# Chunk decays as running products on VectorE, in a kernel of a Mamba-2 scan and an ELU feed-forward layer

## The chip, the cores and the metric

The kernel runs on one core of one Trainium2 chip. The metric is the device time of one execution, in microseconds (us). A core has five engines that run side by side[...]: TensorE (PE in the profile, with its weight loads as PEld), VectorE (DVE), ScalarE (ACT), GpSimd (POOL) and SyncE (SP, which here only issues DMAs). Matmul results go to PSUM.

## The reference

Four batches with eight heads each and 768 tokens pass through a state-space scan; its output, 3072 tokens of 256 features, then passes through a feed-forward layer with ELU. All is float32.

```python
# scan, per batch and head, in chunks (32 tokens here; the result does not depend on the chunk)
la   = log(clip(a, 1e-6, 1));  cum = cumsum(la)          # inside the chunk
L    = exp(cum[i] - cum[j]) * (i >= j)
y    = ((C @ B.T) * L) @ x + (C @ state) * exp(cum)[:, None]
state = exp(sum(la)) * state + sum_j exp(cum[-1] - cum[j]) * B[j] x[j]
# feed-forward
h = y @ w_in;  g = where(h > 0, h, exp(min(h, 0)) - 1);  out = g @ w_out
```

Since cum is a running sum of logarithms, exp(cum[i] - cum[j]) is the product of a over the tokens j+1 to i.

## The kernel before

The sequence is cut into 12 blocks of 256 tokens, numbered n = 0 to 11, and each block into four chunks of 64 tokens (u and v, two by two). A block of the scan needs these steps, whose names recur below:

- `spread_cum` loads, for all eight heads, the row of cum from DRAM (`flat`) into every partition of the tile L (128 partitions are two chunks' tokens j; the free axis is head, u, token i). Its load is one of two buffers of L.
- `decay` turns L in place into decays: an ACT exponent with the bias -cum[j] for each head and u (L439; 16 in a block), and a GpSimd select that zeroes i < j (L444; four in a block). Blocks 0 and 1 make their decays in another way (`first_low`, `first_cum`, `first_decays`) and are not touched by the change.
- `scaled` multiplies B by exp(cum[-1] - cum[j]) on GpSimd; `turn` transposes B and C on TensorE and copies and masks them (ACT `bt`, DVE `ctm` L381, `cts` L389).
- `scores` makes C B^T in four PSUM banks, `weigh` (DVE, L468) multiplies it by L, `sums` and `states` carry the state on, `across` and `inside` make y and copy it to the tile yT.

The float64 weights arrive as raw 32-bit words in 16 pieces and are made into float32: `w_abs` (ACT), `w_low` (an ACT or DVE instruction, the second argument of `w_take` says which), `w_sign` and `w_high` (DVE), `w_sum` (GpSimd).

The feed-forward part of blocks 0 to 3 runs as plain matmuls: `l1` (L583) fills a PSUM bank, `elu` frees it again with ACT Relu (L596), ACT Exp (L603) and the DVE instruction g (L605); `l2` (L707) is the second product. From block 4 on blocks go in pairs (n, n+1), and both products are done by a scheme with seven matrix products in place of eight, which needs additions on DVE and GpSimd. For each pair there are eight rounds i, each of two half-rounds k = 2i and 2i+1:

- even k: `front` (three products into two banks c1 and c2), `front_sums` (DVE L673 and L674; L673 needs the ACT copy L665), the ELU of the c2 before it, with a GpSimd subtraction behind it (`sum_t1`, L727), and four steps of the second product (L759) of the pair before;
- odd k: `mid` (two products), the DVE addition L682, two steps of L759, then `back` (two products; the first overwrites what L682 reads), the DVE additions L689 and L690, one more step of L759, the ELU of c1, and the Relu of c2 begun.

Every fourth step of L759 ends a product, and DVE adds it up (L750). At the end of each half-round `scan_ahead` issues the scan's steps of the pair that comes next: among others `turn` at k = 5 and 7. The whole order is written by hand (`manual_schedule`); each engine executes its own instructions in program order, so an instruction that waits holds all that come behind it on its engine. PSUM is a pool of seven banks used in rotation and one bank of its own.

Of the kernel before, what the change touches and what calls it, by code (L numbers as in the profile page):

```python
# [28 lines left out]
def kernel(  # L29
# [233 lines left out]
    make_heads(0)  # L263
    make_heads(1)

    def clip(t):
        nc.vector.tensor_scalar(
            out=t, in0=t, scalar1=1e-6, scalar2=1.0, op0=ALU.max, op1=ALU.min)
# [26 lines left out]
    nc.scalar.activation(E0, E0, ACT.Exp)  # L295

    F = const.tile([ROWS, 2, 2, P], F32, name="F")
    E = la

    def rest_of_sums():  # L300
        to_last(F[:, 0], E, nc.gpsimd)
        nc.scalar.activation(E, E, ACT.Exp)


    flat = tc.dram_tile([2, ROWS, 2, Q], F32, name="flat")
# [22 lines left out]
    state = {}  # L328
    starts = {}

    def spread_cum(n):
# [27 lines left out]
    def scaled(n, eng):  # L359

        s = st[n]
        s["sc"] = sc = att.tile([P, 2, NH, N], F32, tag="sc", name="sc", bufs=3)
        factor = eb0[:, :, NH * n:NH * (n + 1)] if n < 2 else eb[:, :, rows_of(n)]
        eng.tensor_tensor(
            out=sc, in0=s["bc"][:, 0],
            in1=factor.unsqueeze(3).to_broadcast([P, 2, NH, N]), op=ALU.mult)
# [63 lines left out]

    def decay(n, q):

        decay_of(n, 2 * q)
        decay_of(n, 2 * q + 1)

    def decay_of(n, h):
        L, row = st[n]["L"], rows_of(n).start + NG * h
        for u in range(2):
            nc.scalar.activation(  # L439
                L[:, h, u], L[:, h, u], ACT.Exp, bias=ncum[:, u, row:row + 1])  # L440
        if h % 4 == 3:
            for v in range(2):
                part = L[Q * v:Q * v + Q, h - 3:h + 1]
                nc.gpsimd.affine_select(  # L444
                    out=part, in_=part, pattern=[[0, 4], [0, 2], [1, Q]],
                    compare_op=ALU.is_ge, fill=0.0, base=0, channel_multiplier=-1)

# [387 lines left out]
    states(0, most)  # L835
    w_abs(0)
    w_low(0, nc.scalar)
    log_of(la)
    scores(0)
    idle_product(3)  # L840
    weigh(0, 0)
# [17 lines left out]
    w_high_a(1)  # L859
    w_high_b(1)  # L860
    w_sum(1)
    running_sums(la, F[:, 0], ROWS)
    l1(0, 0)
    w_abs(2)
    w_low(2, nc.scalar)
    w_sign(2)
    w_give(2)
    elu()
    nc.scalar.activation(F[:, 1], F[:, 0], ACT.Exp)
    write_flat()  # L870
    spread_cum(2)
    w_load(5)
    load_bc(2)
    w_load(6)
# [11 lines left out]
    turn(1)  # L886
    first_exp(1)
    scaled(1, nc.gpsimd)
    rest_of_sums()
    w_give(3)  # L890
    make_heads(2)
    turn_exp(1)
    l1(0, 2)
    elu()
# [8 lines left out]
    l1(0, 3)  # L903
    inside(across(1), 1)
    w_take(4, nc.vector)
    ncum = turned(F[:, 0], "ncum", -1.0, nc.vector)
    eb = turned(E, "eb", 1.0, nc.vector)
    w_give(4)
    elu()
    load_bc(3)  # L910
# [3 lines left out]
    for s, (n, i) in enumerate((  # L914
            (1, 0), (1, 1), (1, 2), (0, 4), (1, 3), (0, 5), (1, 4), (0, 6), (1, 5), (0, 7),
            (1, 6), (1, 7))):
        l1(n, i)
        if s < 8:
            decay_of(2, s)
        if s == 7:  # L920
            scores(2)
            weigh(2, 0)
            weigh(2, 1)
        if s % 2 == 1 and todo < 10:
            w_take(todo, nc.vector)
            w_give(todo)
            w_load(todo + 6)
            todo += 1
        if s == 4:
            scaled(2, nc.gpsimd)  # L930
        if s == 5:
            turn(2)
            first_exp(2)
            turn_exp(2)
        if s == 8:
            spread_cum(3)
            load_x(3)
            spread_exp(3)
            weigh(2, 2)
            weigh(2, 3)  # L940

            st[0] = kept
            sums(2, 0, pool=p_o, tag="o", parts=(None, last))
            states(0, last)
            st.pop(0)
            states(2)
        if s == 10:
            spread_cum(4)
            inside(across(2), 2)
        if len(lag) > 1:  # L950
            elu()
# [15 lines left out]
    def scan_ahead(n, i):  # L967


        m = n + 2 + n % 2  # L970
        if 4 < m < NP and n % 2 == 1 and i in (4, 5):
            spread_cum(m + i - 4)
        m = n + 2 - n % 2
        if 4 <= m < NP and n % 2 == 0:
            if i < 2:
                load_bc(m + i)
                spread_exp(m + i)
            if i == 2:
                if m == 4:
                    spread_cum(5)  # L980
                load_x(m)
                load_x(m + 1)
            for k in (i,) if m == 4 else (i, i + 1) if i % 2 == 0 else ():
                if k >= 2:
                    decay(m + k // 6, (k - 2) % 4)
            if i in (5, 7):
                turn(m + i // 7)
                turn_exp(m + i // 7)
        if 4 <= m < NP and n % 2 == 1:
            if i == 0:  # L990
                scaled(m, nc.gpsimd)
                scaled(m + 1, nc.gpsimd)
            for k in (i,) if m == 4 else (i, i + 1) if i % 2 == 0 else ():
                if k < 2:
                    decay(m + 1, k + 2)
            if i == 2 and m == 4:
                scores(m, m + 1)
                sums(m, m + 1)
                for q in range(4):
                    weigh(m, q)  # L1000
                    weigh(m + 1, q)
                states(m)
                states(m + 1)
# [7 lines left out]
    for n in (2, 3):  # L1011
        for i in range(8):
            l2(n - 2, i)
            if todo < len(pieces):
                w_take(todo, nc.vector)
            end_of_two(n, 2 * i)
            l1(n, i)
            if todo < len(pieces):
                w_give(todo)
                w_load(todo + 6)  # L1020
                todo += 1
            while lag:
# [24 lines left out]
            end_of_two(n, 2 * i + 1)  # L1047
# [116 lines left out]
```

## Time and profile before

The time of the kernel is 364.41 us, the median of three runs (364.33 to 365.36). The profiled execution spans 362.9 us, so 1.5 us of the median lie around the span.

| what | value |
|---|---|
| span of the profiled execution | 362.9 us |
| PE busy | 354.3 us (98%) |
| DVE busy | 242.2 us (67%), 547 instructions |
| ACT busy | 200.7 us (55%), 499 instructions |
| POOL busy | 227.1 us (63%), 366 instructions |
| L439, the exponents, ACT 128x64 | 160 instructions, 41.0 us busy, 338 ns each |
| L444, the selects, POOL 64x512 | 40 instructions, 27.3 us busy, 682 ns each |
| DVE g (L605), 128x512 | 96 instructions, 681 ns each |

The busy times of engines other than PE add up work that lies beside PE's, so a smaller sum there need not shorten the span. A matmul's record holds its time in the pipeline, and consecutive matmuls overlap; how fast PE goes is better read from the starts. Three stretches are told apart below: up to 53 us (the first two blocks, the weights arriving, `l1` alone), 53 to 117 us (blocks 2 and 3, `l1` and `l2` in turn), and from 117 us on (the pairs 4, 6, 8 and 10, about 56 us each).

### The profile page before, as it was taken

To read this page: it belongs to the slowest core of one execution; us is meant where nothing else is said; L and a number is where in the kernel's file an instruction comes from. 1 tells how busy PE (TensorE), PEld (TensorE's weight loads), DVE (VectorE), ACT (ScalarE), POOL (GpSimd) and SP (SyncE) were. 2 spreads that over 40 slices of the span, in tenths; PEclk is the share of its full clock that TensorE was granted. 3 is DMA by queue.
4 is the path that set the end of the run, shared out by engine and by line. 5 is a ranking of instruction groups with operands and counts; after the bars stand their busy time and mean duration, and the time that the engine had idled before them with its cause. 6 is when DMAs were issued, how large, how long until landed. Compare 5 with 4: busy or idle time off the path is not lost.

```text
span 362.9 us, 10146 instructions
## 1 busy us (share of the span) xinstructions
PE 354.3 (98%) x3978; PEld 316.9 (87%) x3978; DVE 242.2 (67%) x547; ACT 200.7 (55%) x499; POOL 227.1 (63%) x366
## 2 busy tenths in 40 slices
PE   8899999999999999999999999999999999999996
PEld 5578778888888998898999998999989999999995
DVE  4989887972697668784567684666685666666212
ACT  4858969767435567635485735386735352534100
POOL 4454443663567896679457578567587555456893
PEclk9999999999999999999999999999999999999999
DMA  8877995563050560053530045540000100000001
GB/s 155 203 203 147 240 308 141 66 116 63 3 116 19 65 85 12 4 115 48 96 65 2 3 95 68 93 72 0 3 2 4 58 2 0 3 0 32 29 2 58
DMA packets 96239, 25.33 MB, mean 70 GB/s; under 512 B 77312, under 2 KB 92096, under 8 KB 96192
## 3 DMA queue, kind: packets, MB, share of 16 engines
q1 hardware_dynamic: 94016, 24.49, 33.0%
q8 instruction: 31, 0.51, 0.6%
q10 hardware_dynamic: 2176, 0.20, 0.4%
q14 instruction: 16, 0.13, 0.1%
HBM read 21.33 MB, written 3.34 MB: 68 GB/s over the span
## 4 chain that ended last, share of the span: by engine, by line
PE 81%; DVE 7%; ACT 3%; DMA 3%; SPq 2%; issue 2%; POOL 1%; ACTq 0%; DVEq 0%
PE ps_o L759 32%; PE ps_h L655 25%; PE ps_h L583 10%; PE ps_o L707 8%; SPq L112 2%; PE ps_g L459 1%; DMA w<-in_moe_w_in_dram 1%; DVE g L605 1%; PE ps_y L553 1%; ACT e L596 1%; PE ps_st L489 1%; ACT e L603 1%; DMA flat<-F 1%; DVE mag L183 1%; PE ps_y L534 1%
## 5 line engine op out<-in xcount | busy, mean ns | idle before, releaser
L596 ACT ACTIVATE e<-ps_h 128x512 f32<-128x512 f32 x96 | 56.5, 588 | 93.1 <-DVE ps_h L689 71.2
L605 DVE SCALAR_TENSOR_TENSOR g<-e,ps_h 128x512 f32<-128x512 f32 x96 | 65.3, 681 | 39.2 <-ACT e L603 35.8
L759 PEld LDWEIGHTS ps_o<-w_out,g 128*128 128x128 f32 x640 | 80.3, 192 | 3.3 <-issue 0.5
L759 PE MATMUL ps_o<-w_out,g 128*128 128x128 f32 x640 | 81.4, 275 | 0.0
L727 POOL TENSOR_TENSOR g<-g 128x256 f32<-128x256 f32 x34 | 24.8, 729 | 67.1 <-DVE g L605 67.1
L583 PE MATMUL ps_h<-yT,w_in 128*128 128x256 f32 x256 | 60.6, 383 | 2.5 <-POOL w_in L200 1.8
L603 ACT ACTIVATE e<-e 128x512 f32<-128x512 f32 x96 | 60.9, 634 | 2.2
L583 PEld LDWEIGHTS ps_h<-yT,w_in 128*128 128x128 f32 x256 | 47.8, 190 | 10.6 <-POOL w_in L200 2.8
L759 PE MATMUL ps_o<-w_sum,g 128*128 128x128 f32 x320 | 43.0, 275 | 0.0
L759 PEld LDWEIGHTS ps_o<-w_sum,g 128*128 128x128 f32 x320 | 41.1, 192 | 1.4
L439 ACT ACTIVATE L<-L,ncum 128x64 f32<-128x64 f32 x160 | 41.0, 338 | 0.0
L655 PE MATMUL ps_h<-y_sum,w_in 128*128 128x256 f32 x128 | 38.6, 383 | 0.7 <-DVE ps_h L682 0.7
L655 PE MATMUL ps_h<-y_sum,w_sum 128*128 128x256 f32 x128 | 38.5, 382 | 0.5 <-DVE g L605 0.5
L655 PE MATMUL ps_h<-yT,w_in 128*128 128x256 f32 x128 | 38.8, 385 | 0.0
L444 POOL TENSOR_SCALAR_AFFINE_SELECT L<-L 64x512 f32<-64x512 f32 x40 | 27.3, 682 | 13.1 <-ACT L L439 11.8
L707 PE MATMUL ps_o<-w_out,g 128*128 128x256 f32 x128 | 30.8, 383 | 0.0
L655 PEld LDWEIGHTS ps_h<-y_sum,w_sum 128*128 128x128 f32 x128 | 23.9, 190 | 5.3 <-DVE g L605 1.3
L723 POOL TENSOR_TENSOR g<-t,g 128x256 f32<-128x256 f32 x40 | 27.9, 729 | 0.8 <-PE ps_o L759 0.8
L723 POOL TENSOR_TENSOR t<-g 128x256 f32<-128x256 f32 x40 | 28.1, 736 | 0.2
L723 POOL TENSOR_TENSOR g<-g,t 128x256 f32<-128x256 f32 x40 | 27.9, 730 | 0.2
L707 PEld LDWEIGHTS ps_o<-w_out,g 128*128 128x128 f32 x128 | 23.7, 190 | 3.4 <-POOL L L444 0.2
L689 DVE TENSOR_TENSOR ps_h<-ps_h,u_sum 128x256 f32<-128x256 f32 x32 | 13.7, 429 | 18.3 <-PE ps_h L655 18.3
(109 smaller groups left out, 538.3 us busy)
## 6 DMA issues: line engine op xcount, KB each, us to landing
L<-flat SPq DMA_DIRECT2D x20, 256.0 KB, 5.3
w<-in_moe_w_in_dram SPq DMA_DIRECT2D x8, 512.0 KB, 5.2
w<-in_moe_w_out_dram SPq DMA_DIRECT2D x8, 512.0 KB, 6.1
xr<-in_x_dram SPq DMA_DIRECT2D x24, 128.0 KB, 3.4
out_dram<-c_sum SPq DMA_DIRECT2D x10, 256.0 KB, 2.1
bc<-in_B_dram SPq DMA_DIRECT2D x24, 64.0 KB, 4.4
bc<-in_C_dram SPq DMA_DIRECT2D x22, 64.0 KB, 3.4
ec<-flat_exp SPq DMA_DIRECT2D x72, 16.0 KB, 1.7
```

What stands on the lines that cost most here:

```text
L439: nc.scalar.activation(L[:, h, u], L[:, h, u], ACT.Exp, bias=ncum[:, u, row:row + 1])
L444: nc.gpsimd.affine_select(out=part, in_=part, pattern=[[0, 4], [0, 2], [1, Q]], compare_op=ALU.is_ge, fill=0.0, base=0, channel_multiplier=-1)
L583: nc.tensor.matmul(out=ps[:, j], lhsT=w_in[:, k, m * P:(m + 1) * P], rhs=yT[n // 2][:, k, n % 2].rearrange("p u i -> p (u i)"), start=(k = ...
L596: nc.scalar.activation(begun[0], lag[0][2], ACT.Relu, scale=-1.0)
L603: nc.scalar.activation(e, e, ACT.Exp, scale=-1.0)
L605: nc.vector.scalar_tensor_tensor(out=g_of[n, i], in0=e, scalar=1.0, in1=ps, op0=ALU.subtract, op1=ALU.max)
L655: nc.tensor.matmul(out=out, lhsT=lhsT, rhs=rhs, start=first, stop=True, skip_group_check=True)
L689: nc.vector.tensor_tensor(out=c1[:, 1], in0=c1[:, 1], in1=u[:, 0], op=ALU.add)
L707: nc.tensor.matmul(out=o_of[n][:, ts], lhsT=g_of[n, j][:, m % 2, ts * P:(ts + 1) * P], rhs=w_out[:, m], start=(m == 0 and ts == 0), stop=( ...
L723: nc.gpsimd.tensor_tensor(out=out, in0=in0, in1=in1, op=ALU.subtract)
L727: eng.tensor_tensor(out=b12, in0=b12, in1=g_of[n, i][:, 0], op=ALU.subtract)
L759: nc.tensor.matmul(out=ps[:, ts], lhsT=b[:, ts * P:(ts + 1) * P], rhs=a[:, i], start=(i == chunk[0] and ts == 0), stop=(i == chunk[-1]), s ...
```

## The change

From block 2 on the decays are made without logarithms. The tile L now receives the row of a itself, with a zero at the first token of each chunk, and one DVE scan for each pair of heads makes L[i] = L[i-1] * a[i] + same[i], where `same` is one at i = j and zero elsewhere. So the value is zero before j, one at j, and the product of a from j+1 to i after it; the zero at a chunk's start ends what came before. The last column of L is the factor that `scaled` needs. For all blocks together one scan makes the running products that replace exp(cum).

```diff
+    same = const.tile([P, 4, Q], F32, name="same")
+    def make_same():
+        nc.gpsimd.tensor_tensor(
+            out=same, in0=ident[:, 0:Q].unsqueeze(1).to_broadcast([P, 4, Q]),
+            in1=ident[:, Q:P].unsqueeze(1).to_broadcast([P, 4, Q]), op=ALU.add)
...
-    E = la
-    def rest_of_sums():
-        to_last(F[:, 0], E, nc.gpsimd)
-        nc.scalar.activation(E, E, ACT.Exp)
+    nc.gpsimd.tensor_scalar(
+        out=F[:, 0], in0=keep[0:ROWS], scalar1=-1.0, scalar2=1.0, op0=ALU.mult, op1=ALU.add)
+    def running_products():
+        nc.vector.tensor_tensor_scan(
+            out=F[:, 1].rearrange("p c s -> p (c s)"),
+            data0=F[:, 0].rearrange("p c s -> p (c s)"),
+            data1=la.rearrange("p c s -> p (c s)"), initial=0.0, op0=ALU.max, op1=ALU.mult)
+        nc.gpsimd.tensor_tensor(out=F[:, 0], in0=la, in1=keep[0:ROWS], op=ALU.mult)
...
-        factor = eb0[:, :, NH * n:NH * (n + 1)] if n < 2 else eb[:, :, rows_of(n)]
+        factor = (eb0[:, :, NH * n:NH * (n + 1)] if n < 2 else
+                  s["L"][:, :, :, Q - 1].rearrange("p h u -> p u h"))
...
     def decay(n, q):
-        decay_of(n, 2 * q)
-        decay_of(n, 2 * q + 1)
-    def decay_of(n, h):
-        L, row = st[n]["L"], rows_of(n).start + NG * h
-        for u in range(2):
-            nc.scalar.activation(
-                L[:, h, u], L[:, h, u], ACT.Exp, bias=ncum[:, u, row:row + 1])
-        if h % 4 == 3:
-            for v in range(2):
-                part = L[Q * v:Q * v + Q, h - 3:h + 1]
-                nc.gpsimd.affine_select(
-                    out=part, in_=part, pattern=[[0, 4], [0, 2], [1, Q]],
-                    compare_op=ALU.is_ge, fill=0.0, base=0, channel_multiplier=-1)
+        part = st[n]["L"][:, 2 * q:2 * q + 2].rearrange("p k u i -> p (k u i)")
+        nc.vector.tensor_tensor_scan(
+            out=part, data0=part, data1=same.rearrange("p k i -> p (k i)"),
+            initial=0.0, op0=ALU.mult, op1=ALU.add)
...
-    log_of(la)
...
-    running_sums(la, F[:, 0], ROWS)
+    running_products()
...
-    nc.scalar.activation(F[:, 1], F[:, 0], ACT.Exp)
     write_flat()
-    spread_cum(2)
+    spread_a(2)
...
-    rest_of_sums()
     w_give(3)
     make_heads(2)
+    make_same()
...
-    ncum = turned(F[:, 0], "ncum", -1.0, nc.vector)
-    eb = turned(E, "eb", 1.0, nc.vector)
...
-        if s < 8:
-            decay_of(2, s)
+        if s in (1, 3, 5, 6):
+            decay(2, (s + 1) // 2 - 1 if s < 6 else 3)
...
-            w_take(todo, nc.vector)
+            w_take(todo, nc.scalar)
...
-        if s == 4:
+        if s == 6:
             scaled(2, nc.gpsimd)
...
-            for k in (i,) if m == 4 else (i, i + 1) if i % 2 == 0 else ():
-                if k >= 2:
-                    decay(m + k // 6, (k - 2) % 4)
+            if m > 4:
+                decay(m + i // 4, i % 4)
+            elif i >= 2:
+                decay(m + i // 6, (i - 2) % 4)
...
             if i == 0:
                 scaled(m, nc.gpsimd)
+            if m == 4 and i < 2:
+                decay(m + 1, i + 2)
+            if i == (1 if m == 4 else 0):
                 scaled(m + 1, nc.gpsimd)
-            for k in (i,) if m == 4 else (i, i + 1) if i % 2 == 0 else ():
-                if k < 2:
-                    decay(m + 1, k + 2)
...
-                w_take(todo, nc.vector)
+                w_take(todo, nc.scalar)
```

`spread_cum` is renamed `spread_a` in all its places. In `scan_ahead` the variable i is the half-round k for pairs up to k = 7, so the eight scans of a coming pair stand at the end of k = 0 to 7, one in each; `w_take(..., nc.scalar)` moves `w_low` of the weight pieces 5 to 15 from DVE to ACT. The DMAs that SyncE issues are the same, in the same order.

More of the change, by code (lines that the diff above doesn't have):

```diff
@@ L329, with spread_a @@
     starts = {}
-    def spread_cum(n):
+    def spread_a(n):
         st.setdefault(n, {})["L"] = L = att.tile([P, NH, 2, Q], F32, tag="L", name="L", bufs=2)
@@ L935 @@
         if s == 8:
-            spread_cum(3)
+            spread_a(3)
             load_x(3)
@@ L947 @@
         if s == 10:
-            spread_cum(4)
+            spread_a(4)
             inside(across(2), 2)
@@ L971, in scan_ahead @@
         if 4 < m < NP and n % 2 == 1 and i in (4, 5):
-            spread_cum(m + i - 4)
+            spread_a(m + i - 4)
         m = n + 2 - n % 2
@@ L979, in scan_ahead @@
                 if m == 4:
-                    spread_cum(5)
+                    spread_a(5)
                 load_x(m)
                 load_x(m + 1)
-            for k in (i,) if m == 4 else (i, i + 1) if i % 2 == 0 else ():
-                if k >= 2:
-                    decay(m + k // 6, (k - 2) % 4)
+            if m > 4:
+                decay(m + i // 4, i % 4)
+            elif i >= 2:
+                decay(m + i // 6, (i - 2) % 4)
             if i in (5, 7):
```

## The prediction
> **What bounds the kernel now.** I read the page first: its busy times, then the chain that ended last.
>
> ```profile
> PE 354.3 (98%) x3978; PEld 316.9 (87%) x3978; DVE 242.2 (67%) x547; ACT 200.7 (55%) x499; POOL 227.1 (63%) x366
> PE 81%; DVE 7%; ACT 3%; DMA 3%; SPq 2%; issue 2%; POOL 1%; ACTq 0%; DVEq 0%
> ```
>
> TensorE is the chain. That its 98% are real work must be read from the starts, so next the chain in order of time, here two rounds of pair 6:
>
> ```profile
> 180.41 1.30 PE ps_h L655 x6
> 181.71 1.78 PE ps_o L759 x16
> 183.50 0.87 PE ps_h L655 x4
> 184.36 0.89 PE ps_o L759 x8
> 185.25 0.87 PE ps_h L655 x4
> 186.12 0.44 PE ps_o L759 x4
> 186.56 1.30 PE ps_h L655 x6
> ```
>
> A round takes 6.15 us without a gap. In PE's timeline a 128x256 record follows the one before by 0.216 us and a 128x128 record by 0.111; where starts lie further apart than their count gives, PE waited. Outside the first 27 us such waits of 0.3 us or more are only at 42.4 (0.8), 51.3 (0.4), 140.5 (0.8), 167.3 (0.5), 222.9 (0.5) and 264.8 (0.3): 3.3 us in all, the most that any relief of ACT or POOL can return there. So the question is what the change does to DVE, which feeds PE. The timeline of DVE in the same round, then of POOL:
>
> ```profile
> 181.34 0.69 DVE L605 SCALAR_TENSOR_TENSOR g<-e,ps_h 128x512 f32<-128x512 f32 x1 [0.90 <-ACT e L603]
> 182.08 0.42 DVE L673 TENSOR_TENSOR u_sum<-ps_h,p_copy 128x256 f32<-128x256 f32 x1
> 182.54 0.42 DVE L674 TENSOR_TENSOR u_sum<-ps_h,u_sum 128x256 f32<-128x256 f32 x1
> 182.88 0.68 DVE L605 SCALAR_TENSOR_TENSOR g<-e,ps_h 128x512 f32<-128x512 f32 x1
> 183.48 0.42 DVE L750 TENSOR_TENSOR c_sum<-ps_o,p_sum 128x256 f32<-128x256 f32 x1
> 184.40 0.43 DVE L682 TENSOR_TENSOR ps_h<-ps_h,u_sum 128x256 f32<-128x256 f32 x1 [0.51 <-PE ps_h L655]
> 185.72 0.43 DVE L689 TENSOR_TENSOR ps_h<-ps_h,u_sum 128x256 f32<-128x256 f32 x1 [0.89 <-PE ps_h L655]
> ```
>
> ```profile
> 183.64 0.73 POOL L727 TENSOR_TENSOR g<-g 128x256 f32<-128x256 f32 x1 [2.68 <-DVE g L605]
> 184.32 2.79 POOL L723 TENSOR_TENSOR g<-g,t 128x256 f32<-128x256 f32 x4
> ```
>
> This is a loop: PE's `back`, L689, Relu and Exp on ACT, g(c1), L673, L674, g(c2), L750, L682, and the next `back`, which overwrites what L682 read. Its slack in this round: 0.14 us before L673 (it could follow g by 0.60), 0.58 before L682 (it could follow L750 by 0.34), and 0.22 on PE (`back` starts at 185.09 by PE's timeline, L682 ends at 184.83, the hand-over takes 0.04): 0.94 us. DVE looks 67% busy, but the idle time of this loop is mostly the wait for ACT (0.90), and that wait is inside the loop.
>
> The rows that price the change, from the groups kept apart by shape, and two instructions of DVE and POOL near 130 us:
>
> ```profile
> L439 ACT ACTIVATE L<-L,ncum 128x64 f32<-128x64 f32 x160 | 41.0, 338 | 0.0
> L274 DVE TENSOR_TENSOR_SCAN F<-keep,la 128x256 f32<-128x256 f32 x1 | 0.7, 691 | 0.5 <-ACT la L271 0.5
> ```
>
> ```profile
> 129.80 0.76 DVE L631 TENSOR_TENSOR w_sum<-w_out 128x128 f32<-128x128 f32 x1
> 130.59 0.63 DVE L631 TENSOR_TENSOR w_sum<-w_out,w_sum 128x128 f32<-128x128 f32 x1
> ```
>
> ```profile
> 127.62 2.79 POOL L723 TENSOR_TENSOR g<-g,t 128x256 f32<-128x256 f32 x4
> 130.36 1.45 POOL L444 TENSOR_SCALAR_AFFINE_SELECT L<-L 64x512 f32<-64x512 f32 x2
> ```
>
> **What the Trainium skill says.** "SBUF — State Buffer", Who interferes with whom: a DVE instruction with two SBUF inputs contends with a GpSimd instruction that reads SBUF, and the second to issue fully blocks until the first is finished. The trace agrees: L631 has two SBUF inputs and takes 0.28 us at its shortest, but at 129.80 it takes 0.76, ending 0.2 to 0.3 after POOL's L723 does. The scan has two SBUF inputs too. "Perfetto Trace Analysis", Identifying the Most-Contended Engine, warns that matmul busy time says little; here the starts settle it. No page prices the scan; the trace has one of the same shape.
>
> **Start to 27 us.** Removed: Ln of la (0.42), Exp of F (0.40) and Exp of E (0.42) on ACT, the subtraction on POOL (0.61), two transposed tables (0.56 of PE from 26.99 on, two DVE copies of 0.38). Added: on POOL the constant F[:, 0] in a 2.40 us hole before 7.10, its product (0.61 by the removed row) after `w_sum` ends at 17.07, so before 18.41, when SyncE, held by a weight load until then, issues `flat`; and `same` (0.73 by the 128x256 rows) between 23.50 and 24.63, where POOL waits. The scan over all blocks replaces one of equal size. SyncE's queue keeps its order, its spread waits for `flat` to land at 21.96 as before, and no DMA moves. The tables' PE time lay under ACT's copies of yT, which end at 27.50, with `l1` at 27.55. `scaled` reads its factor from L with a stride in place of a table, taken at its old 655 ns. The freed ACT lets a g at 22.47 start some 0.3 earlier. Gain 0 to 0.3, hidden at the next wait.
>
> **27 to 53 us.** `w_low` leaves DVE (0.58 each) for ACT (0.77), four scans come to DVE, 16 exponents leave ACT (0.25 each by their spacing). The PE wait at 42.4 ends with a g at 43.07, in a chain that begins when a weight lands at 35.14. From there ACT loses six exponents (1.5) and gains two `w_low` (1.3): equal. DVE's second half gets dense: behind the g at about 38.85 stand a scan, three weight instructions (1.4), ctm, cts, g, another scan, each by its spacing: 38.85 + 0.60 + 0.60 + 1.40 + 0.93 + 0.60 + 0.60 = 43.6 instead of 43.07, so PE loses 0.5. The removed `w_low` of the next piece lets `states` run 0.4 earlier against PE, and PE waited 0.4 for them at 50. Net +0.1, between -0.5 and +0.6.
>
> **53 to 117 us.** PE has no gap. Per round DVE trades a `w_low` for a scan or two (+0.1 to +0.8), and there are 3.46 us of PE per round with several banks between. The weight pieces must be ready for `l2` (slack about 0.5 us at 68.8), but L444 and the exponents leave ACT and POOL ahead of them, so they come no later. A scan that waits for its L would hold DVE; the loads land 5.3 us after issue at the median, and all are issued before. Zero; at worst +1.
>
> **Pairs 4, 6 and 8.** Here lies the cost. The scan of an odd k stands between g(c1) and L673, that of an even k right before L682: both in the loop, while the exponents they replace stood behind ACT's Exp, and the selects off it. Each scan costs 0.60 by start-to-start spacing (the 96x256 scan at 14.95 is followed at 15.55). It cannot cost less than 0.34, the spacing of plain 128x256 additions, nor more than 0.60 and one whole POOL instruction, 0.73; I take the scan's own row. That of an even k meets L727: POOL starts it 0.76 after g(c2) starts and keeps it to about 1.44; the scan, behind L750, is ready at 0.94, so it waits 0.50. For pair 6:
> - k = 0: DVE idles 0.84 before L682; hidden.
> - Round 0 to 1: 0.60 + 0.60 + 0.50 = 1.70 against 0.94 of slack: +0.76.
> - Round 1 to 2: the same rows (g 187.48, L750 189.63, L682 190.55): +0.76, sum 1.5.
> - Round 2 to 3: `turn` stands in the loop (ctm, cts), L682 at 197.18 waits for nothing; slack only 0.21. POOL's addition, delayed by the scan, holds an L750 and with it L689 by 0.1 more: 1.70 + 0.10 - 0.21 = +1.6, sum 3.1.
> - Round 3 to 4: one scan (0.60) against 0.80 of slack: 0.
>
> Behind that, no scan; PE is dense and returns nothing. Pair 8 has the same rows 55.6 us later: 3.1. Pair 4 has DVE's L631 in addition, and its L689 was late by a POOL backlog that the removed selects shorten; working the same rows through gives 3.2; I take 3.1. Pair 10 has no scans. Sum 3 x 3.1 = 9.3.
>
> **Sum.** Against the profiled span: 362.9 + 0.1 + 9.3 = 372.3; with the 1.5 around it, 373.8 us, +2.6% on the median of 364.41.
>
> **Rivals.**
> - *Scans do not block* (or fall between POOL's instructions). For: POOL is 63% busy only. Against: L727 is released by the very g that the scan follows. Then rounds cost 0.26, 0.26 and 0.99, 1.5 a pair: 4.5 + 0.1, so 369.0.
> - *Faster: relief of ACT and POOL wins.* If a scan costs DVE under 0.4, two fit into 0.94, and the waits at 42.4, 51.3 and 140.5 (2.0) go, with 0.3 at the start: 362.1. Against: the trace has 0.69 for this shape. The point is the loop's slack of 0.94 a round.
> - *Worse: DVE so late that PE also waits for PSUM banks*, as it did for a g at 167.3, or that scans wait for L: another 1 a pair and 1 in the middle, 377.8.
> - *The scan is placed elsewhere than the source reads*: the instruction order shows them where I count them; dropped.
>
> **How the numbers follow.** Blocked loop 0.58, unblocked 0.20, worse 0.12, faster or hidden 0.10. The likeliest alone reaches from 371 to 376 (blocking 0.3 to 0.6 a scan). Leaving out the faster case and the far end of the worse one gives 366.5 to 378. The measurement can tell 0.3%, about 1.1 us. Slower takes all but the last case and a little of the second: 0.88; faster 0.07, same 0.05.
>
> **What would show it.** DVE scans of 0.69 us, longer ones beside L727; in pairs 4, 6 and 8 the rounds 0 to 3 at 6.9, 6.9 and 8.2 us (before 6.15, 6.15 and 6.6), PE's `back` waiting for DVE L682; from round 4 on spacing as before. ACT near 167 us busy (200.7 less 41.0 and 1.2, plus 11 x 0.77) and POOL near 201 (less 27.3, plus 1.4), without effect. Wrong if these rounds stay at 6.15, or if the time before 117 us moves by over 1.

## The result, and the profile after

The changed kernel takes 374.95 us (median of four runs, 374.40 to 375.93) where the kernel before takes 364.37 (four runs, 364.06 to 365.36): a ratio of 1.0286, with a 95% interval from 1.0262 to 1.0310. The predicted time was 373.8 us. The profiled execution spans 373.2 us, 10.3 more than before.

The page's busy times, and the chain that ended last by engine:

```profile
PE 357.1 (96%) x3974; PEld 318.9 (85%) x3974; DVE 261.8 (70%) x574; ACT 169.3 (45%) x347; POOL 206.2 (55%) x328
PE 67%; DVE 15%; POOL 6%; ACT 5%; issue 4%; DMA 1%; SPq 1%; POOLq 0%; DVEq 0%; ACTq 0%
```

ACT lost 31 us of work and POOL 21, and the kernel got slower: neither was what bounded it. The chain's share of DVE went from 7% to 15%, and PE's from 81% to 67%. The groups kept apart by shape give the scan's price, and the waits (in all, times, longest, in us) what PE now waits for:

```profile
L446 DVE TENSOR_TENSOR_SCAN L<-L,same 128x256 f32<-128x256 f32 x40 | 34.1, 856 | 0.0
PE ps_h L657 <- DVE ps_h L684: 6.9, 9, 1.5
PEld ps_st L491 <- POOL sc L376: 2.1, 7, 0.4
```

Nine waits of PE's `back` for L684 are three pairs times three rounds. DVE's timeline shows how one of them comes about, here round 0 to 1 of pair 6 (start, duration; in brackets the idle time before it):

```profile
185.30 0.69 DVE L607 SCALAR_TENSOR_TENSOR g<-e,ps_h 128x512 f32<-128x512 f32 x1 [0.89 <-ACT e L605]
185.91 0.68 DVE L446 TENSOR_TENSOR_SCAN L<-L,same 128x256 f32<-128x256 f32 x1
186.51 0.40 DVE L675 TENSOR_TENSOR u_sum<-ps_h,p_copy 128x256 f32<-128x256 f32 x1
186.94 0.42 DVE L676 TENSOR_TENSOR u_sum<-ps_h,u_sum 128x256 f32<-128x256 f32 x1
187.28 0.68 DVE L607 SCALAR_TENSOR_TENSOR g<-e,ps_h 128x512 f32<-128x512 f32 x1
187.88 0.42 DVE L752 TENSOR_TENSOR c_sum<-ps_o,p_sum 128x256 f32<-128x256 f32 x1
188.21 1.10 DVE L446 TENSOR_TENSOR_SCAN L<-L,same 128x256 f32<-128x256 f32 x1
189.23 0.40 DVE L684 TENSOR_TENSOR ps_h<-ps_h,u_sum 128x256 f32<-128x256 f32 x1
```

PE's and POOL's timelines in the same round:

```profile
189.69 0.70 PE L657 MATMUL ps_h<-y_sum,w_in 128*128 128x256 f32 x2 [0.46 <-DVE ps_h L684]
```

```profile
188.03 0.73 POOL L729 TENSOR_TENSOR g<-g 128x256 f32<-128x256 f32 x1 [2.79 <-DVE g L607]
```

From the first g on DVE does not pause: eight instructions follow each other up to L684. The odd scan takes 0.60 by its start-to-start time. The even one, behind POOL's L729, takes 1.02 (188.21 to 189.23), so 0.42 of waiting. L684 ends at 189.63 and `back` starts at 189.69.

In PE's timeline the starts of `back` measure every round. The table gives where the first `back` of pair 4 starts in the profiled execution, the sum of rounds 0 to 3 of two pairs (us), and the experiments told of below; each ratio is to the kernel before on the same chip in the same set of runs. Pairs 6 and 8 agree to 0.02 us in every kernel; the first `back` is one execution's, and executions of one kernel differ by 1 us and more.

| kernel | first back | pair 4 | pair 6 | time, us | ratio (95%) |
|---|---|---|---|---|---|
| before | 122.24 | 26.64 | 25.47 | 364.37 | |
| changed | 123.47 | 29.15 | 28.25 | 374.95 | 1.0286 (1.0262 to 1.0310) |
| e1_no_scans | 121.82 | 25.56 | 25.47 | 364.90 | 0.9999 (0.9980 to 1.0019) |
| e2_scan_first | 122.64 | 28.19 | 27.35 | 371.29 | 1.0168 (1.0120 to 1.0216) |
| e3_holes | 122.12 | 27.85 | 25.46 | 367.03 | 1.0066 (1.0050 to 1.0081) |
| e4_wlow_only | 124.03 | 26.64 | 25.47 | 367.32 | 1.0060 (1.0043 to 1.0076) |
| e5_turn_first | 122.44 | 27.86 | 25.47 | 366.02 | 1.0034 (1.0019 to 1.0048) |
| e6_spread | 126.26 | 27.57 | 25.46 | 369.44 | 1.0132 (1.0103 to 1.0161) |
| e7_wlow_dve | 122.25 | 29.16 | 28.27 | 373.83 | 1.0257 (1.0226 to 1.0288) |
| e8_gap | 122.38 | 27.20 | 25.47 | 365.54 | 1.0005 (0.9987 to 1.0023) |
| e9_g_first | 123.11 | 27.21 | 25.46 | 365.31 | 1.0012 (0.9999 to 1.0025) |
| e10_odd_only | 122.83 | 26.99 | 26.15 | 368.26 | 1.0086 (1.0058 to 1.0114) |
| e11_relief | 121.75 | 25.72 | 25.46 | 363.97 | 0.9978 (0.9962 to 0.9993) |
| e12_before_relief | 124.83 | 25.46 | 25.47 | 363.51 | 0.9966 (0.9949 to 0.9983) |

The kernel before took 364.60 us beside e1 to e4, 364.48 beside e5 to e7, 365.04 beside e8 to e10 and 364.75 beside e11 and e12.

The 10.3 us of span fall apart thus: 1.23 up to the first `back`, nearly all of it one wait of PE near 64 us (block 3's turn, below); rounds 0 to 3 of pairs 4, 6 and 8 with 2.51, 2.78 and 2.79, together 8.08; round 4 to 5 of the same pairs with 0.24, 0.25 and 0.22 (in pair 6 from 9.06 to 9.31), together 0.71; 0.27 at the end. Pair 10, without scans, has its rounds as before.

### The profile page after: what moved, and what is told of

It is laid out like the page before. It is cut to its first block, busy times and chain, and to the rows that moved or that the text cites. A ratio compares the mean times of both kernels' runs of the same rounds, so it can differ in the third digit from the quotient of the medians.

```text
span 373.2 us, 9971 instructions
## 1 busy us (share of the span) xinstructions
PE 357.1 (96%) x3974; PEld 318.9 (85%) x3974; DVE 261.8 (70%) x574; ACT 169.3 (45%) x347; POOL 206.2 (55%) x328
## 4 chain that ended last, share of the span: by engine, by line
PE 67%; DVE 15%; POOL 6%; ACT 5%; issue 4%; DMA 1%; SPq 1%; POOLq 0%; DVEq 0%; ACTq 0%
PE ps_o L761 23%; PE ps_h L657 18%; PE ps_h L585 11%; PE ps_o L709 7%; DVE L L446 4%; DVE g L607 3%; POOL g L725 2%; ACT e L598 2%; ACT e L605 2%; POOL p_sum L752 1%; DVE ps_h L691 1%; PE ps_y L555 1%; DMA w<-in_moe_w_in_dram 1%; DVE c_sum L752 1%; SPq L112 1%
## 5 line engine op out<-in xcount | busy, mean ns | idle before, releaser
L729 POOL TENSOR_TENSOR g<-g 128x256 f32<-128x256 f32 x34 | 25.3, 745 | 85.4 <-DVE g L607 85.4
L585 PEld LDWEIGHTS ps_h<-yT,w_in 128*128 128x128 f32 x256 | 49.1, 194 | 9.9 <-POOL w_in L200 1.8
L657 PE MATMUL ps_h<-y_sum,w_in 128*128 128x256 f32 x128 | 39.4, 389 | 6.9 <-DVE ps_h L684 6.9
L446 DVE TENSOR_TENSOR_SCAN L<-L,same 128x256 f32<-128x256 f32 x40 | 34.1, 856 | 0.0
L709 PE MATMUL ps_o<-w_out,g 128*128 128x256 f32 x128 | 30.8, 383 | 0.0
L657 PEld LDWEIGHTS ps_h<-y_sum,w_in 128*128 128x128 f32 x128 | 21.8, 190 | 10.4 <-DVE ps_h L684 8.6
L725 POOL TENSOR_TENSOR g<-g,t 128x256 f32<-128x256 f32 x40 | 29.0, 754 | 0.0
L725 POOL TENSOR_TENSOR g<-t,g 128x256 f32<-128x256 f32 x40 | 28.2, 736 | 0.8 <-PE ps_o L761 0.8
L725 POOL TENSOR_TENSOR t<-g 128x256 f32<-128x256 f32 x40 | 27.9, 729 | 0.0
L709 PEld LDWEIGHTS ps_o<-w_out,g 128*128 128x128 f32 x128 | 23.7, 190 | 3.4 <-issue 0.2
L691 DVE TENSOR_TENSOR ps_h<-ps_h,u_sum 128x256 f32<-128x256 f32 x32 | 13.7, 429 | 17.9 <-PE ps_h L657 17.8
```

Of the source, the lines that this page charges most:

```text
L446: nc.vector.tensor_tensor_scan(out=part, data0=part, data1=same.rearrange("p k i -> p (k i)"), initial=0.0, op0=ALU.mult, op1=ALU.add)
L585: nc.tensor.matmul(out=ps[:, j], lhsT=w_in[:, k, m * P:(m + 1) * P], rhs=yT[n // 2][:, k, n % 2].rearrange("p u i -> p (u i)"), start=(k = ...
L657: nc.tensor.matmul(out=out, lhsT=lhsT, rhs=rhs, start=first, stop=True, skip_group_check=True)
L691: nc.vector.tensor_tensor(out=c1[:, 1], in0=c1[:, 1], in1=u[:, 0], op=ALU.add)
L709: nc.tensor.matmul(out=o_of[n][:, ts], lhsT=g_of[n, j][:, m % 2, ts * P:(ts + 1) * P], rhs=w_out[:, m], start=(m == 0 and ts == 0), stop=( ...
L725: nc.gpsimd.tensor_tensor(out=out, in0=in0, in1=in1, op=ALU.subtract)
```

## The experiments

Two theories about the rounds are to be told apart. The prediction's: the scans stand in DVE's part of the loop, and those of even k are also held by L729. The rivals: the scans do not block, or something else of the change (the freed ACT and POOL, `w_low` on ACT) makes the rounds late.

**No scans in the pairs.** e1_no_scans leaves the scans of blocks 6 to 11 out, 24 of 40, so it does not compute the decays of these blocks.

```diff
-            if m > 4:
-                decay(m + i // 4, i % 4)
-            elif i >= 2:
+            if m == 4 and i >= 2:
                 decay(m + i // 6, (i - 2) % 4)
```

> The changed kernel with the scans of pairs 6, 8 and 10 left out (24 of 40; L keeps the raw rows of a, so the decays of these blocks are not computed). If the scans in the DVE loop cost the time: the rounds 0 to 3 of pairs 4, 6 and 8 go back to 6.15, 6.15 and 6.6 us, and the time falls by the 7.9 us that these rounds lost and most of the 0.9 lost behind them, to 366 to 367 us. If something else of the change costs it (the copies of the weights on ACT, the strided factor, the order of the queues): it stays above 372.

Measured: 364.90 us, level with the kernel before; rounds of 6.15, 6.15, 6.58 and 6.59 in pair 6, as before. So with these 24 scans the whole loss goes, within the error. Pair 4 is even 1.1 faster than before in its rounds: round 2 to 3 takes 6.59 where the kernel before had 7.66, since PE no longer waits for L682 there. PE's timeline before, then in e1_no_scans:

```profile
142.20 0.70 PE L655 MATMUL ps_h<-y_sum,w_in 128*128 128x256 f32 x2 [0.67 <-DVE ps_h L682]
```

```profile
140.70 0.69 PE L657 MATMUL ps_h<-y_sum,w_in 128*128 128x256 f32 x2
```

With the selects gone (two of them, 1.45 us, stood at 130.36) POOL's p_sum, which this round needs, ends at 134.10 instead of 136.01; e12_before_relief below brings the same round to 6.59 by relieving POOL alone. The expectation of 366 to 367 counted only what the changed kernel had lost against the kernel before, and left this 1.1 out. In pair 4 the scans therefore cost 3.6 (29.15 less 25.56), and the relief of POOL gave 1.1 of it back.

**The even scan ahead of L752.** e2_scan_first puts it behind the g of c2, so that DVE is in the scan when POOL wants to start L729.

```diff
                     next_elu()
+                    if m and k < 8:
+                        decay(m + k // 4, k % 4)
                     l2s(2)
```

> The changed kernel with the scan of an even half-round moved up by a DVE addition: straight behind g(c2), ahead of L752, so that it starts before POOL's L729 does. If the scan is held by L729: the even scans take 0.69 instead of 1.10 us, the three lengthened rounds of each pair become shorter by some 0.4 each, 9 x 0.4 = 3.7, and the time is near 371.3. If the long scans have another reason, or POOL's own lateness then matters as much: 374 to 375.

Measured: 371.29 us, pair 6's rounds at 6.36, 6.45, 7.86 and 6.68. First DVE's, then POOL's timeline of the changed order:

```profile
185.51 0.68 DVE L607 SCALAR_TENSOR_TENSOR g<-e,ps_h 128x512 f32<-128x512 f32 x1
186.10 0.68 DVE L446 TENSOR_TENSOR_SCAN L<-L,same 128x256 f32<-128x256 f32 x1
186.71 0.40 DVE L752 TENSOR_TENSOR c_sum<-ps_o,p_sum 128x256 f32<-128x256 f32 x1
187.02 0.42 DVE L684 TENSOR_TENSOR ps_h<-ps_h,u_sum 128x256 f32<-128x256 f32 x1
```

```profile
186.26 1.04 POOL L729 TENSOR_TENSOR g<-g 128x256 f32<-128x256 f32 x1 [2.79 <-DVE g L607]
```

The scan is back at 0.68, and now L729 takes 1.04 instead of 0.73: whichever comes second waits. Taking the block away from DVE makes a round of pair 6 0.42 shorter twice (6.78 to 6.36, 6.87 to 6.45), the very time that the scan had waited. In round 2 to 3 next to nothing is won: POOL is late there, and an L752 waits 0.59 for its p_sum. That the time is the 371.3 expected is therefore partly luck: the rounds of the three pairs became 2.8 us shorter, not 3.7, and the other 0.8 lies ahead of the first `back` (122.64 after 123.47), where executions scatter.

**Odd scans alone.** e10_odd_only leaves out the 12 scans of even k, so it too does not compute all decays.

```diff
             if m > 4:
-                decay(m + i // 4, i % 4)
+                if i % 2:
+                    decay(m + i // 4, i % 4)
```

> The changed kernel with the scans at even k of pairs 4, 6 and 8 left out (12 of 40: pair heads 0 and 2 of each coming block), so that those heads' decays of blocks 6 to 11 are not made; the scans at odd k stay where the change put them, between g and L675. The prediction gave the loop 0.94 us of slack in rounds 0 to 2 and 0.21 in round 2 to 3. By it one scan of 0.60 costs nothing in the first two rounds and 0.4 in round 2 to 3: rounds of pair 6 and 8 at 6.15, 6.15, 6.9 to 7.0, 6.6, and 366 to 367 in all. Rival (DVE or GpSimd has no such slack, each scan costs its own length): rounds of 6.75, 6.75, 7.2, 369 or more.

Measured: pair 6's rounds at 6.15, 6.15, 7.16 and 6.69. A scan of 0.60 a round is free in the first two rounds, as it should be with a slack of 0.94, and costs 0.58 where the slack is 0.21. DVE's timeline in round 0 to 1 of pair 6 shows what is left of the slack:

```profile
182.54 0.69 DVE L607 SCALAR_TENSOR_TENSOR g<-e,ps_h 128x512 f32<-128x512 f32 x1 [0.89 <-ACT e L605]
183.15 0.69 DVE L446 TENSOR_TENSOR_SCAN L<-L,same 128x256 f32<-128x256 f32 x1
...
185.12 0.42 DVE L752 TENSOR_TENSOR c_sum<-ps_o,p_sum 128x256 f32<-128x256 f32 x1
185.61 0.43 DVE L684 TENSOR_TENSOR ps_h<-ps_h,u_sum 128x256 f32<-128x256 f32 x1
```

L684 follows L752 by 0.49, where 0.34 is the shortest, so 0.15 is left there; and `back` starts at 186.30, 0.26 after L684 ends, so another 0.22. Together that is 0.37, and 0.94 less 0.60 is 0.34. The time is 368.26 rather than 366 to 367: against the kernel before, rounds 0 to 3 lost 1.7 in the three pairs instead of 1.2 (0.35 in pair 4 and 0.68 in each of the others), round 4 to 5 kept its 0.25 a pair, and the wait for block 3's turn (below) is in it too.

**The same scans in holes.** e3_holes keeps all 40. In each pair one stands at the end of k = 0, three between L684 and L691, and four behind L692, so behind the instructions that PE waits for.

```diff
                 l2s(2)
+                if m and i in (0, 1, 3):
+                    later()
                 back(n, i)
+                if m and i < 4:
+                    later()
```

Here `later()` makes the next scan of the pair.

> The same 40 scans, but those of pairs 6, 8 and 10 stand where DVE waits: the first at the end of k = 0 as before, three between L684 and L691 (DVE waits 0.8 to 0.9 us for PE there), four behind L692 (0.9 us of wait for ACT). If it is the place in the loop that costs: rounds back to 6.15, 6.15 and 6.6 us but for some 0.3 where POOL holds a scan, time 366 to 368. If it is the amount of DVE work or the contention with POOL wherever it falls: rounds stay long, time above 372.

Measured: 367.03 us. In pair 6 the rounds are those of the kernel before to 0.01 us, with all eight scans in them: position, not the sum of DVE's work, was the cost. What is left in the rounds is in pair 4, whose rounds 1 to 2 and 2 to 3 take 6.51 and 8.50. There DVE and POOL have weight sums (L633) as well. DVE's timeline, then POOL's:

```profile
134.30 0.42 DVE L684 TENSOR_TENSOR ps_h<-ps_h,u_sum 128x256 f32<-128x256 f32 x1
136.07 0.42 DVE L752 TENSOR_TENSOR c_sum<-ps_o,p_sum 128x256 f32<-128x256 f32 x1 [1.35 <-POOL p_sum L752]
136.41 0.41 DVE L752 TENSOR_TENSOR p_sum<-ps_o,p_sum 128x256 f32<-128x256 f32 x1
136.75 0.42 DVE L691 TENSOR_TENSOR ps_h<-ps_h,u_sum 128x256 f32<-128x256 f32 x1
```

```profile
128.30 3.62 POOL L725 TENSOR_TENSOR g<-g,t 128x256 f32<-128x256 f32 x4
131.88 0.50 POOL L633 TENSOR_TENSOR w_sum<-w_in 128x128 f32<-128x128 f32 x1
...
133.95 1.41 POOL L729 TENSOR_TENSOR g<-g 128x256 f32<-128x256 f32 x2
135.31 0.72 POOL L752 TENSOR_TENSOR p_sum<-p_sum 128x256 f32<-128x256 f32 x1
```

POOL works without a pause from 128 on; four L725 take 3.62 beside the scans, against 2.79 without. p_sum comes late, DVE waits 1.35 for it, and behind this L752 stands L691, which the loop needs.

**`w_low` alone.** e4_wlow_only is the kernel before with one part of the change: `w_low` of pieces 5 to 15 on ACT (in both calls `w_take(todo, nc.vector)` becomes `w_take(todo, nc.scalar)`).

> The kernel before with one part of the change alone: w_low of the weight pieces 5 to 15 on ACT in place of DVE. Prediction's reading: no more than 0.5 us either way, 364 to 365, since the PE wait at 42.4 hangs on ACT and DVE alike and PE has no gap from 53 to 117. Rival, that the move to ACT is what the first 117 us lose (1.2 us in the changed kernel): 365.5 or more, the exponents of L being still on ACT here.

Measured: 367.32 us, 0.6% slower, and the rival's reason is seen. ACT has no pause from 35.7 to 47 us, exponents (L439) and `w_low` (L164) in one row; the Relu L596 that starts at 41.80 before starts at 43.00; its g waits 0.93 for ACT, and PE 0.94 for this g. ACT, DVE and PE in that order:

```profile
40.17 0.76 ACT L164 ACTIVATE w_in<-w,two 128x512 f32<-128x512 uint32 x1
...
43.00 0.57 ACT L596 ACTIVATE e<-ps_h 128x512 f32<-128x512 f32 x1
43.61 0.63 ACT L603 ACTIVATE e<-e 128x512 f32<-128x512 f32 x1
```

```profile
44.27 0.69 DVE L605 SCALAR_TENSOR_TENSOR g<-e,ps_h 128x512 f32<-128x512 f32 x1 [0.93 <-ACT e L603]
```

```profile
45.01 1.99 PE L583 MATMUL ps_h<-yT,w_in 128*128 128x256 f32 x8 [0.94 <-DVE g L605]
```

The first `back` comes 1.8 later than before, and no pair changes.

**`w_low` back.** e7_wlow_dve is the changed kernel with this part undone (the same two calls, the other way).

> The changed kernel with one part undone: w_low of weight pieces 5 to 15 is back on VectorE. In e4_wlow_only the move of w_low to ScalarE alone, with the exponents still there, cost 2.4 us of span before pair 4 and nothing after. Theory: with the exponents gone ScalarE has the room and VectorE, with four scans more, does not, so that undoing it costs: gaps on PE at 43 us and near 51, first back of pair 4 later by 0.5 to 2, time 375.0 to 377.0 (the changed kernel 374.9), pair rounds as in the changed kernel. Rival (w_low on ScalarE is a loss in any company): 373.0 to 374.4.

Measured: 373.83 us. Its time lies in the rival's range, but the rival's mechanism is not there: the first `back` starts at 122.25, and the executions with `w_low` on ACT and the same code up to there (the changed kernel, e1, e2, e3, e10) have 121.82 to 123.47. The ratios of the two overlap, and of the 1.1 us between the medians a part is the clock (last section): three of four executions of the changed kernel had it lowered, none of the six of e7_wlow_dve; the one without took 374.40. With the exponents gone ACT has the room, and where `w_low` stands no longer matters to what these runs can tell; the theory that DVE would lack it fell.

**Block 3's turn.** The changed kernel and e1, e2, e3, e7 and e10 have a wait of PE at 62 to 65 us that the kernel before has not. In the changed kernel, DVE's timeline, then PE's, and last the same matmul in the kernel before:

```profile
62.19 0.68 DVE L607 SCALAR_TENSOR_TENSOR g<-e,ps_h 128x512 f32<-128x512 f32 x1
62.79 2.04 DVE L446 TENSOR_TENSOR_SCAN L<-L,same 128x256 f32<-128x256 f32 x2
64.75 0.66 DVE L393 TENSOR_TENSOR ctm<-ps_tc,hmask 128x512 f32<-128x512 f32 x1
```

```profile
65.56 0.70 PE L461 MATMUL ps_g<-ctm,bt 32*64 32x128 f32 x32 [1.06 <-DVE ctm L393]
```

```profile
64.43 0.69 PE L459 MATMUL ps_g<-ctm,bt 32*64 32x128 f32 x32
```

ctm stands behind two scans of its own block, where exponents on ACT stood beside it. The first product L709 of `l2` still starts at 53.53, as before (L707, 53.54), so the 1.13 us between the two matmuls arise after that point. e5_turn_first is e3_holes with `turn` and `turn_exp` of block 3 ahead of its last two scans.

```diff
-                if i < 2:
-                    decay(3, 2 * i)
-                    decay(3, 2 * i + 1)
                 if i == 1:
-                    scaled(3, nc.gpsimd)
                     turn(3)
                     turn_exp(3)
+                if i < 2:
+                    decay(3, 2 * i)
+                    decay(3, 2 * i + 1)
+                if i == 1:
+                    scaled(3, nc.gpsimd)
```

> e3_holes with one edit more: block 3's turn (transposes, bt, ctm, cts) stands ahead of its last two scans instead of behind all four. In e3_holes PE stood still for 0.82 us at 61.5, waiting for ctm behind these scans. Theory (in-order DVE: the scans hold ctm up): the gap at 61 us goes or halves, the first back of pair 4 comes 0.5 to 0.9 earlier relative to the l1 at 50 us, all rounds from there as in e3_holes; time 366.2 to 366.6 where e3_holes had 367.0. Rival (something else is late there too, such as the copy bt on ACT or the L of block 3): the gap stays at 0.5 or more under another name, time as e3_holes.

Measured: PE is busy for all of the 64 us from 53 to 117 again (63.2 in e3_holes), and the ratio is 1.0034 after 1.0066; 366.02 us is a little under the 366.2 to 366.6 expected. The two ran on different chips and their intervals lie side by side (1.0019 to 1.0048, 1.0050 to 1.0081), so that the wait is gone is read from the trace.

**Pair 4, three steps.** e6_spread moves block 6's scans to the end of block 3's feed-forward and puts none behind L692 in pair 4.

```diff
+            if i == 7 and m == 4:
+                for q in range(4):
+                    decay(6, q)
             if i == 2 and m == 4:
```

> e5_turn_first with pair 4's scans spread out: those of block 6 move to the end of block 3's feed-forward, where VectorE idles for 2.9 us (115.5 to 118.5 in e1_no_scans) and L has landed; block 7's four stand at the end of k = 0 and between L684 and L691 of rounds 0, 1 and 3; none behind L692 in this pair. In e3_holes pair 4's rounds 1 and 2 took 6.51 and 8.50 us (e1_no_scans, without any scan there: 6.15 and 6.59); scans lengthened the weight sums L633 and GpSimd's additions L725, until a VectorE addition L752 waited 1.35 us for GpSimd. Theory (contention through GpSimd's backlog): rounds 0 to 3 come down to 6.15, 6.15, 6.6 to 7.2, 6.7, and the time to 363.7 to 364.8, level with the kernel before or below it by up to 0.3%. Rival (the scans between L684 and L691 alone suffice to delay GpSimd): round 2 stays at 8 or more, 365.5 to 366.5.

Measured: 369.44 us, a miss of my own making. The four scans came behind the last g of block 3 instead of into the idle time before it (DVE's timeline, then PE's):

```profile
119.18 0.69 DVE L607 SCALAR_TENSOR_TENSOR g<-e,ps_h 128x512 f32<-128x512 f32 x1 [2.92 <-ACT e L605]
119.78 4.25 DVE L446 TENSOR_TENSOR_SCAN L<-L,same 128x256 f32<-128x256 f32 x4
```

```profile
126.26 0.85 PE L657 MATMUL ps_h<-y_sum,w_in 128*128 128x256 f32 x2 [3.58 <-DVE ps_h L684]
```

Four scans took 4.25 us beside POOL's L725, 1.06 each. e8_gap puts three of them ahead of this g.

```diff
+            if (n, i) == (3, 7):
+                for q in range(3):
+                    decay(6, q)
             while lag:
                 elu()
```

> e5_turn_first with pair 4's scans spread out again, now in the right place: three of block 6 stand ahead of the last g of block 3 (in e6_spread they stood behind it, and PE waited 3.58 us), where VectorE idles for 2.9 us; the other five at the end of k = 0, between L684 and L691 of rounds 0, 1 and 3, and behind L692 of round 3. In e6_spread rounds 1 to 3 of pair 4 were 6.15, 6.85 and 6.68 (e5_turn_first: 6.51, 8.51, 6.69). Theory: rounds 0 to 3 of 6.15, 6.15, 6.85, 6.69, no new gap at 118 to 123 of more than 0.5, so 1.5 to 2.2 off e5_turn_first's 366.0: 363.8 to 364.6, level with the kernel before. Rival (the scans lengthen y_sum on GpSimd, which front needs): a gap of 1 or more near 119 to 123, 365 or more.

Measured: no wait at 118 to 123, rounds of 6.15, 6.15, 8.21: the first part held, the second did not. 365.54 us, level with the kernel before (ratio 1.0005) though not below it. In round 2 to 3 DVE's L752 waited 1.92 for POOL's p_sum, with POOL's weight sums right ahead of it:

```profile
136.34 0.42 DVE L752 TENSOR_TENSOR c_sum<-ps_o,p_sum 128x256 f32<-128x256 f32 x1 [1.92 <-POOL p_sum L752]
```

```profile
133.80 0.46 POOL L633 TENSOR_TENSOR w_sum<-w_in,w_sum 128x128 f32<-128x128 f32 x1
134.21 1.41 POOL L729 TENSOR_TENSOR g<-g 128x256 f32<-128x256 f32 x2
135.58 0.73 POOL L752 TENSOR_TENSOR p_sum<-p_sum 128x256 f32<-128x256 f32 x1
```

e9_g_first is e8_gap with block 2's four scans behind the g of their step (the two `if` parts with `decay(2, ...)` and `scaled(2, ...)` moved below `elu()`).

> e8_gap with one edit more: in the stretch from 27 to 53 us the four scans of block 2 (and its scaled, which needs them) stand behind the g of the same step, not ahead of it. In e5_turn_first PE stood still for up to 1.4 us at 42.4, with a scan at 43.10 right ahead of the g that it waited for (43.70). Theory (in-order VectorE, one scan ahead of g is 0.6): the gap comes down by about 0.6, and the time by 0.3 to 0.7, to 363.3 to 364.0. Rival (the arrival of the weight piece sets this g, not the scan): the gap stays, time as e8_gap within 0.2.

Measured: 365.31 us, ratio 1.0012, not to be told from e8_gap; the 363.3 to 364.0 of the theory did not come. The wait at 42 to 43 us is 0.5 us in it, but among executions with one code in this stretch (e1, e3, e5 and e8) it varies from under 0.3 to 1.4; what sets it is open.

e11_relief is e8_gap with POOL's last two sets of weight sums in rounds 2 and 3.

```diff
                     if i < 2:
-                        sum_weights(nc.gpsimd, a_in, s_in, 6 + i)
                         sum_t1(2, 6 + i)
+                    else:
+                        sum_weights(nc.gpsimd, a_in, s_in, 4 + i)
```

> e8_gap with GpSimd's last weight sums (L633, 2.0 us in each of two rounds of pair 4) moved from rounds 0 and 1 to rounds 2 and 3. In e8_gap round 2 to 3 of pair 4 still took 8.21 us, because a VectorE addition L752 waited 1.92 us for GpSimd's p_sum, which stood behind these sums at 132.2 to 134.2; GpSimd idles from 139 on. Theory (the rest of the cost in pair 4 is GpSimd's backlog): this round falls to 6.6 to 7.0, time 1.2 to 1.6 below e8_gap's 365.5, that is 363.9 to 364.3 where the kernel before has 365.0, a ratio of 0.997 to 0.998. Rival (something else is as late, such as the copies on ScalarE or a bank of PSUM): the round stays above 7.6.

Measured: round 2 to 3 of pair 4 at 6.59 us, 363.97 us, a ratio of 0.9978 (0.9962 to 0.9993): all 40 scans are in, and of the versions that make every decay in the new way it is the fastest. A part of the win is paid back behind it: round 3 to 4 takes 6.83 and round 4 to 5 9.54, in e8_gap 6.69 and 9.19. Whether that is the change's gain is shown by the same edit on the kernel before:

> The kernel before with the same move of GpSimd's weight sums alone, to see whose gain that is. Its round 2 to 3 of pair 4 takes 7.66 us where pairs 6 and 8 take 6.58, with PE waiting 0.67 us for L682 at 140.5. Theory: here too the backlog of GpSimd is the cause, the round falls to 6.6 to 6.8 and the time by 0.8 to 1.1 us, a ratio of 0.997 to 0.998, so that e11_relief gains nothing on a kernel before that is mended in the same way. Rival (the selects L444, which only this kernel has, fill GpSimd in rounds 2 and 3, so that the sums are as late there): no change, ratio 0.999 to 1.001.

Measured: that round falls from 7.66 to 6.59, and the ratio is 0.9966. (In its profiled execution PE once waited 2.25 us at 85 us, for a late load of L that held ACT; only the rounds are read from it.) The intervals of the two overlap: with the scans in the right places the new decays are neither faster nor slower than the old, as far as these runs can tell. By the rounds they are 0.7 behind in pair 4 (6.83 and 9.54 in the two rounds named, where e12_before_relief has 6.58 and 9.07).

## Why the prediction was right

The sign and the size held: 373.8 said, 374.95 measured, inside both ranges. So did the mechanism: `back` waits for L684 in the nine rounds named, and the scans ahead of L684 are what delays it (e1_no_scans, e10_odd_only, e3_holes). That the sum came so near is partly luck: the rounds were put 1.2 us too high, and three terms put at nothing or left out cost 2.1 together (1.1 by block 3's turn, 0.7 in round 4 to 5, 0.3 at the end). Point by point:

- *Price of the scan*: 0.69 us said, the shortest 0.66 and 0.68 where nothing disturbs, 0.60 from start to start. Right.
- *The block by L729*: 0.50 said, 0.42 measured (1.02 less 0.60). Right in kind; e2_scan_first shows it as the cause. The Trainium skill, "SBUF — State Buffer", Who interferes with whom, calls the port pair that DVE and GpSimd share an exclusive lock: whoever issues first has it for the whole instruction, and the other fully blocks. The runs agree that either side can be the one that waits, but for less than the whole overlap of the records: L729 runs from 188.03 to 188.76 and the scan's turn came at 188.21, so a full block would be 0.55. The prediction's own example reads the same way: L631 ends at 130.56, 0.15 after L723 (130.41) and not 0.2 to 0.3, so it waited 0.48 of an overlap of 0.61.
- *Slack of the loop*: 0.94 in two rounds, 0.21 in the third. e10_odd_only confirms both in sign: free, free, 0.58 (0.39 by the prediction).
- *Rounds*: 6.9, 6.9 and 8.2 said; 6.78, 6.87 and 7.91 in pair 6. The sum of 9.3 was too large by 1.2 (8.08): 0.3 in each of pairs 6 and 8, where the block's 0.08 in three rounds is most of it, and 0.6 in pair 4, which was not worked out for itself and cost 0.62, 1.23 and 0.65 in the three rounds rather than 0.76, 0.76 and 1.6. Round 3 to 4 cost 0.10 instead of 0 in pairs 6 and 8.
- *"Behind that, no scan; PE is dense and returns nothing"* failed by 0.24 a pair: the scan at the end of k = 7 is hidden for PE but, by the traces, not for POOL. In round 4 of pair 6 POOL's subtraction L729 starts 0.53 ahead of `back` (210.63 and 211.16), before 1.04 ahead (L727 at 203.37, `back` at 204.41), so L725 and `scaled` behind it are later, and `sums` wait 0.4 for sc. The kernels with no scan at the end of k = 7 (e1_no_scans and e3_holes) have 9.07 us there in pair 6, as before. No run moves this scan alone, and pair 4 of e3_holes keeps 0.11 of its loss without it, so the cause is likely rather than shown.
- *"53 to 117 us: Zero"* failed. I had added up DVE's work for a round and not asked what stood behind the scans: ctm did, and PE waits 0.8 to 1.1 us for it, the bad end that the text allowed. e5_turn_first shows it. By the prediction's own sign ("wrong if the time before 117 us moves by over 1") this part was wrong: it moved by 1.23.
- *Start to 53 us*: +0.1 said. In the two profiles the first product of `l2` starts at 53.53 and 53.54, so this stretch lost nothing, and the +1.23 is the wait for ctm but for 0.1. Executions of one code differ by more than that: e1_no_scans, e2_scan_first, e3_holes and e10_odd_only, the same code up to there, start this product at 52.09 to 52.95, and the changed kernel's profile is one with a lowered clock (last section). So the stretch may have gained half a microsecond or more; with one profile of the kernel before the size stays open. The claim that ACT's gain and `w_low` balance is right in the part that could be tested: `w_low` alone costs (e4_wlow_only), with the exponents gone it does not (e7_wlow_dve).
- *ACT near 167, POOL near 201 busy, without effect*: 169.3 and 206.2. "Without effect" holds but for pair 4's round 2 to 3, where e1_no_scans shows that the relief of POOL takes 1.1 us off; it is the wait at 140.5 that the prediction's "faster" rival named, and in the changed kernel the scans hide it. POOL is above its number because its own instructions got longer beside the scans (p_sum L752 from 726 to 840 ns).

The rival that scans do not block would have given 369.0 us; e2_scan_first, which takes the block off DVE, gives 371.29, since POOL pays for it in round 2 to 3 and block 3's turn stays late.

## What to carry to other kernels

Moving work off two engines that are half idle onto a third gains nothing by the sum of busy times; what counts is what stands behind each new instruction in program order on its engine, and whether that engine is inside a loop that feeds TensorE. The relief itself pays only where a step waits for the freed engine's backlog (1.1 us in pair 4 here). Work that nobody awaits for a while belongs behind the instruction that releases TensorE, not before it: in pairs 6 and 8 the same 16 scans cost 5.6 us ahead of it and nothing behind it. When an addition loses to a backlog elsewhere, look for a piece of work without a near due date in that backlog, and try the same mend on the kernel before.

## What the hardware showed beside this

DVE and POOL hold each other up, and it acts on both sides: the scan went from 0.68 to 1.10 us when L729 came first, L729 from 0.73 to 1.04 when the scan did, and four L725 from 2.79 to 3.62. In a kernel where both are busy, DVE's work therefore lengthens POOL's queue too.

From start to start a scan of 128x256 takes 0.60 us (185.91 to 186.51) where a plain addition of this shape takes 0.34 (186.94 to 187.28).

TensorE's granted clock fell for a moment near the start in some executions and not in others. The windows of the changed kernel (busy times of the engines, the clock, the DMA share and GB/s), and one of the kernel before:

```profile
14.00:16.00 2.00, 2.00 (x6) 1.64 (x5) 1.97 (x3) 1.48 (x3) 0.85 (x2) 0.50 0.56 53
16.00:18.00 2.00, 2.00 (x39) 1.24 (x38) 1.97 (x4) 0.84 (x2) 2.00 (x2) 0.78 0.95 226
```

```profile
14.00:16.00 2.00, 1.89 (x25) 1.30 (x32) 1.97 (x5) 1.92 (x4) 0.85 (x2) 1.00 0.58 66
```

The second `l1` starts at 18.74 in the changed kernel, at 17.13 in the kernel before. Of the experiments' profiles e6, e8 and e9 show the fall too (0.83 on average from 10 to 20 us). It is not made good later: the first product of `l2` starts at 53.53 to 54.31 in these four profiles, a mean of 53.8 (53.6 without e9, whose order differs from 27 us on), and at 52.09 to 53.64, a mean of 52.8, in the six others with the changed code up to there (e1, e2, e3, e5, e10, e11). The mean clock of an execution tells the two kinds apart, 0.995 or less with the fall and 0.998 or more without it in the profiles. Of 163 executions of the kernel before that were run beside the experiments, 45 had 0.995 or less, with a median of 365.32 us; the other 118 had 364.45. So some 0.9 us go with the fall, and a comparison of a few executions can carry that much: all six of e6_spread had it. What sets it off is open.
